# Turning keys in place on VectorE, with zero-padded query weights, in a two-layer decode kernel

## The chip, the cores and the metric

The kernel runs on one core of one Trainium2 chip. The metric is the device time of one execution in microseconds (us), given as the median of several runs. A profile of one execution is shown beside it. In the profile PE is the matrix engine (PEld its weight loads), DVE is VectorE, ACT is ScalarE, POOL is GpSimd and SP is SyncE, which here only issues DMA transfers. "Span" is the profiled execution from its first to its last recorded event.

## The reference, cut to what matters

Two attention blocks and two feed-forward blocks alternate on four tokens (batch B = 4, one position each). The key and value caches are by far the largest operands: 4 x 8 heads x 8192 positions x 128 numbers in bf16, 64 MB for each, and each is read once per attention block.

```python
def _A_ref(x, k_cache, v_cache, wq, wo):          # B=4, Sq=1, D=512, Hq=32, Hkv=8, Sk=8192, Dh=128
    q = (x @ wq).reshape(B, Sq, Hq, Dh).transpose(0, 2, 1, 3)
    k = jnp.repeat(k_cache, 4, axis=1)
    v = jnp.repeat(v_cache, 4, axis=1)
    scores = jnp.einsum("bhqd,bhkd->bhqk", q, k) * (Dh ** -0.5)
    p = _softmax(scores, axis=-1)
    o = jnp.einsum("bhqk,bhkd->bhqd", p, v)
    return o.transpose(0, 2, 1, 3).reshape(B, Sq, Hq * Dh) @ wo
...
x = x + _A_ref(_layernorm(x), A_k_cache, A_v_cache, A_wq, A_wo)
x = x + _B_ref(_layernorm(x), B_w_gate, B_w_up, B_w_down)     # silu(x@wg) * (x@wu) @ wd
x = x + _A_ref(_layernorm(x), A_k_cache, A_v_cache, A_wq, A_wo)
x = x + _B_ref(_layernorm(x), B_w_gate, B_w_up, B_w_down)
```

## The kernel before

**Units.** One unit u is a pair of a key/value head and a batch entry (32 units in each of two layers). Its keys are 8192 x 128 numbers and make one transfer of 2 MB into one of six slots of the tile kv; its values make another. In a slot, partition p holds 64 consecutive positions, so column block t (of 64, 128 columns each) is a 128 x 128 matrix with positions on the partitions. Eight column blocks make one of the eight blocks q of a unit.

**Loads.** All transfers are issued by SP (line 93) in the order of load_order: K0, K1, V0, K2, V1, ... K29, V28, K30, K31, V29, V30, V31, then the same for the second layer. The weights of the output projection and of the feed-forward block are put between the first loads. pump issues a load as soon as a slot is free, and finished, called after the last use of a slot, frees it: so a transfer waits until PE has done its last matmul on an older one. Only the very last V is cut into four transfers with semaphores of their own.

**One unit.** A score is a sum over the 128 head dimensions, so these must lie on the partitions of both operands. Per block q, transposes (line 292) turns eight 128 x 128 matrices by PE matmuls against the identity into a PSUM bank, and DVE (line 299) or ACT (line 301), in turn, copies the 128 x 1024 result over the keys in the slot. scores (line 311) then does eight matmuls, one for each column block, with the turned keys as weights and q as the moving operand, 32 columns wide, of which four count. The scores of a unit fill 256 columns of one bank: partition = position within a block, columns = (t, head). The softmax follows in steps: maximum per partition and head on DVE (line 318), a transpose and a second maximum (max_t, lines 323 to 327), the maximum spread to all partitions by a matmul and subtracted by DVE (max_b, lines 334 to 338), exp on ACT (line 340), and the sum by a matmul with ones, a DVE sum and a reciprocal (lsum, lines 344 to 349). pv (line 358) does 64 matmuls with the values as weights and the exponentials as the moving operand, and DVE multiplies by the reciprocal of the sum (line 364). Every fourth unit, out_proj (line 377) adds four heads' share to x.

**Order.** Every engine takes its instructions in the order in which the program gives them. attention(L) writes that order by hand: in step (u, q) PE does the transposes of block q of unit u, the scores of block q-2, one step of the softmax of unit u-1 at q = 2, 4 and 7, a quarter of the pv of unit u-1 at q = 7, and the other three quarters of unit u-2 at q = 0, 1, 2. So the values of unit u are used during the steps of units u+1 and u+2.

**Between the layers.** center and deviation are the layer norm, ffn the feed-forward block, qproj the query projection (line 416, 128 matmuls), which ends with a DVE multiplication that writes qT (line 422). Nothing of the next layer's keys is touched by an engine before qproj is issued.

Of the kernel before, what the change touches and what calls it, by code (L numbers as in the profile page):

```python
# [103 lines left out]
def bass_interleave_layers__gqa_block_cached__swiglu_ffn__decode_kernel(  # L104
# [25 lines left out]
    NB = TT // TB  # L130
    NQ = 4
# [5 lines left out]
    ALL = range(NB)  # L137

    with ExitStack() as es:
# [9 lines left out]
        ones_bf = sb("ones_bf", [P, P], BF16)  # L149
        onesf = sb("onesf", [P, P], FP32)  # L150
        xio = sb("xio", [B, D], BF16)
# [11 lines left out]
        qT = sb("qT", [P, B * Hq + WIDE], BF16)  # L163
        oT = sb("oT", [P, Hq, B], BF16)
        mx = sb("mx", [P, REP], FP32)
        m4 = sb("m4", [REP, 1], FP32)
        dg = sb("dg", [REP, REP], FP32)
        mb = sb("mb", [P, REP], FP32)
        pT = sb("pT", [P, 2, TT * REP + WIDE], BF16)
        lt = sb("lt", [P, REP], FP32)  # L170
        rl = sb("rl", [P, 2, REP], FP32)
        eg = sb("eg", [P, FO * B], FP32)
        rg = sb("rg", [P, FO * B], FP32)
        gr = sb("gr", [P, FO * B], FP32)
        gw = sb("gw", [P, FO * B], FP32)
        hT = sb("hT", [P, FO * B], BF16)
        xoT = sb("xoT", [P, XB], BF16)

# [10 lines left out]
        STG = [2, 3, 4]  # L189
        OBK = [5, 6]  # L190
        MISC = 7
# [19 lines left out]
        T.op("pool", lambda e: e.memset(onesf[:], 1.0), writes=["onesf"])  # L211
        T.op("pool", lambda e: e.memset(ones_bf[:], 1.0), writes=["ones"])
        T.op("dve", lambda e: e.memset(eps_sb[:], EPS), writes=["eps"])
        T.op("dve", lambda e: e.memset(lsc_sb[:], math.log(scale)), writes=["lsc"])
        T.op("dve", lambda e: e.memset(zero_sb[:], 0.0), writes=["zero"])
        T.op("dve", lambda e: e.tensor_copy(identf[:], ident[:]), reads=["ident"], writes=["identf"])
        T.op("dve", lambda e: e.memset(qT[:, B * Hq:], 0.0), writes=["qpad"])
        T.op("dve", lambda e: e.memset(pT[:, :, TT * REP:], 0.0), writes=["pT0", "pT1"])
        nc.scalar.preload_act_table_set("natural_log_exp_and_others")

# [33 lines left out]
        def pump():  # L254
            while issued[0] < len(items) and free:
# [8 lines left out]
                if items[n] == ("V", 1, NU - 1):  # L264
                    w = TT * Dh // NQ
                    n8 = NB // NQ
                    for q in range(NQ):
                        T.dma("sp", kv[:, s, q * w:(q + 1) * w], src[:, q * w:(q + 1) * w], sem_l[q],
                              writes=[f"s{s}.{q * n8 + k}" for k in range(n8)])
                else:  # L270
                    T.dma("sp", kv[:, s, :], src, sem_s[s], writes=[f"s{s}.{q}" for q in ALL])
# [7 lines left out]
        evac_n = [0]  # L279
        EVAC = ["dve", "act"]  # L280
        stg_n = [0]

        def transposes(L, u, blocks):
            s = slot_of["K", L, u]
            for q in blocks:
                bk = STG[stg_n[0] % len(STG)]
                stg_n[0] += 1
                stg = bank_bf(bk)
                key = f"s{s}.{q}"
                for t in range(TB):  # L290
                    c = (q * TB + t) * Dh
                    T.op("pe", lambda e: e.matmul(stg[:, t * P:(t + 1) * P], lhsT=kv[:, s, c:c + Dh], rhs=ident[:],  # L292
                                                  is_transpose=True, start=True, stop=True),
                         reads=[key, "ident"], writes=[f"pb{bk}"], sig=(t == TB - 1))
                dst = kv[:, s, q * TB * Dh:(q + 1) * TB * Dh]
                eng = EVAC[evac_n[0] % len(EVAC)]
                evac_n[0] += 1
                if eng == "dve":
                    T.op("dve", lambda e: e.tensor_copy(dst, stg[:, :]), reads=[f"pb{bk}"], writes=[key])  # L299
                else:  # L300
                    T.op("act", lambda e: e.activation(dst, stg[:, :], ACTF.Copy), reads=[f"pb{bk}"], writes=[key])  # L301


        def scores(L, u, q):
            g, b = unit_gb(u)
            s = slot_of["K", L, u]
            bk = SBK[u % 2]

            c0 = b * Hq + g * REP
            for t in range(q * TB, (q + 1) * TB):  # L310
                T.op("pe", lambda e: e.matmul(bank(bk)[:, t * REP:t * REP + WIDE], lhsT=kv[:, s, t * P:(t + 1) * P],  # L311
                                              rhs=qT[:, c0:c0 + WIDE], start=True, stop=True),
                     reads=[f"s{s}.{q}", "qpad"] + [f"q{g}" for g in range(G)], writes=[f"pb{bk}"],
                     sig=(t % TB == TB - 1))
            if q == NB - 1:
                finished(("K", L, u))
                v = bank(bk)[:, 0:TT * REP].rearrange("p (t h) -> p h t", h=REP)
                T.op("dve", lambda e: e.tensor_reduce(mx[:], v, AX.X, ALU.max), reads=[f"pb{bk}"], writes=["mx"])  # L318

        mbank = bank(MISC)  # L320

        def max_t(u):
            T.op("pe", lambda e: e.matmul(mbank[0:REP, 0:P], lhsT=mx[:], rhs=identf[:], is_transpose=True,  # L323
                                          start=True, stop=True),
                 reads=["mx", "identf"], writes=["pb7"])
            T.op("dve", lambda e: e.tensor_reduce(m4[:], mbank[0:REP, 0:P], AX.X, ALU.max), reads=["pb7"], writes=["m4"])  # L326
            T.op("dve", lambda e: e.tensor_scalar(dg[:], identf[0:REP, 0:REP], m4[:, 0:1], None, op0=ALU.mult),  # L327
                 reads=["m4", "identf"], writes=["dg"])

        def max_b(u):  # L330
            bk = SBK[u % 2]
            sc = bank(bk)[:, 0:TT * REP]
            sc3 = sc.rearrange("p (t h) -> p t h", h=REP)
            T.op("pe", lambda e: e.matmul(mbank[:, 0:REP], lhsT=onesf[0:REP, :], rhs=dg[:], start=True, stop=True),  # L334
                 reads=["dg", "onesf"], writes=["pb7"])
            T.op("dve", lambda e: e.tensor_copy(mb[:], mbank[:, 0:REP]), reads=["pb7"], writes=["mb"])
            m3 = mb[:].unsqueeze(1).to_broadcast([P, TT, REP])
            T.op("dve", lambda e: e.tensor_tensor(sc3, sc3, m3, ALU.subtract),  # L338
                 reads=[f"pb{bk}", "mb"], writes=[f"pb{bk}"])
            T.op("act", lambda e: e.activation(pT[:, u % 2, 0:TT * REP], sc, ACTF.Exp),  # L340
                 reads=[f"pb{bk}"], writes=[f"pT{u % 2}"])

        def lsum(u):
            T.op("pe", lambda e: e.matmul(mbank[:, 0:TT * REP], lhsT=ones_bf[:], rhs=pT[:, u % 2, 0:TT * REP],  # L344
                                          start=True, stop=True),
                 reads=[f"pT{u % 2}", "ones"], writes=["pb7"])
            T.op("dve", lambda e: e.tensor_reduce(lt[:], mbank[:, 0:TT * REP].rearrange("p (t h) -> p h t", h=REP),  # L347
                                                  AX.X, ALU.add), reads=["pb7"], writes=["lt"])
            T.op("dve", lambda e: e.reciprocal(rl[:, u % 2, :], lt[:]), reads=["lt"], writes=[f"rl{u % 2}"])  # L349


        def pv(L, u, blocks):
            g, b = unit_gb(u)
            s = slot_of["V", L, u]
            bk = OBK[u % 2]

            for t in range(blocks[0] * TB, (blocks[-1] + 1) * TB):
                T.op("pe", lambda e: e.matmul(bank(bk)[:, 0:WIDE], lhsT=kv[:, s, t * Dh:(t + 1) * Dh],  # L358
                                              rhs=pT[:, u % 2, t * REP:t * REP + WIDE],
                                              start=(t == 0), stop=(t == TT - 1)),  # L360
                     reads=[f"s{s}.{t // TB}", f"pT{u % 2}"], writes=[f"pb{bk}"], sig=(t % TB == TB - 1))
            if blocks[-1] == NB - 1:
                finished(("V", L, u))
                T.op("dve", lambda e: e.tensor_tensor(oT[:, g * REP:(g + 1) * REP, b], bank(bk)[:, 0:REP],  # L364
                                                      rl[:, u % 2, :], ALU.mult),
                     reads=[f"pb{bk}", f"rl{u % 2}"], writes=["oT"])


        def add_to_x():
            T.op("dve", lambda e: e.tensor_tensor(xT[:], xT[:], mbank[:, 0:XB], ALU.add),  # L370
                 reads=["x", "pb7"], writes=["x"])

        def out_proj(g):
            for nt in range(KT):
                for r in range(REP):
                    h = g * REP + r
                    T.op("pe", lambda e: e.matmul(mbank[:, nt * B:(nt + 1) * B],  # L377
                                                  lhsT=wo_sb[:, h, nt * P:(nt + 1) * P], rhs=oT[:, h, :],
                                                  start=(r == 0), stop=(r == REP - 1)),
                         reads=[f"wo{h // (Hq // 4)}", "oT"], writes=["pb7"], sig=(r == REP - 1))  # L380
# [6 lines left out]
        def center():  # L387
            T.op("dve", lambda e: e.tensor_reduce(xs[:], xT[:].rearrange("p (k b) -> p b k", b=B), AX.X, ALU.add),
                 reads=["x"], writes=["xs"])
            T.op("pe", lambda e: e.matmul(mbank[:, 0:B], lhsT=onesf[:], rhs=xs[:], start=True, stop=True),  # L390
# [153 lines left out]
```

## Time and profile before

| | us |
|---|---|
| median of 3 runs | 708.73 (706.93 to 709.47) |
| the profiled execution | 707.09 |
| its span | 705.3 |
| PE busy | 560.2 (79% of the span) |
| DVE busy | 317.8 (45%) |
| ACT busy | 280.3 (40%) |
| POOL busy | 1.0 |
| HBM read | 282.33 MB, 400 GB/s over the span |
| idle of ACT before the copies of line 301 | 322.4, ended by the transposes |
| idle of DVE before the copies of line 299 | 237.2, ended by the transposes |

How to read it: the profiled execution is 1.8 us longer than its span and 1.6 us shorter than the median. "Busy" is time with a recorded instruction; a busy PE need not be at its peak, since matmuls overlap. The page also cuts the span into 40 slices of 17.6 us and gives for each the bytes moved per second; other views answer for any stretch of time, listing for each engine its busy time, the clock granted to PE (1.00 is full) and the mean busy share of the 16 DMA engines.

### The profile page before, as it was taken

How to read it: one execution, taken by the hardware profiler on the slowest of the kernel's cores; microseconds unless marked ns; L12 is line 12 of the kernel's file. 1: busy time of each engine (PE TensorE's matmuls, PEld its weight loads, DVE VectorE, ACT ScalarE, POOL GpSimd, SP SyncE). 2: the span in 40 equal slices, each digit the busy share in tenths (PEclk: the TensorE clock that was granted, in tenths of full speed). 3: DMA queues.
4: the chain of work that ended last, by engine and by line, in shares of the span. 5: the costliest groups of instructions: out<-in, count | busy, mean ns of one | idle time of the engine just before them, and what ended most of it. 6: DMA issues, size and time to landing. Idle time of an engine off the chain costs nothing.

```text
span 705.3 us, 28511 instructions
## 1 busy us (share of the span) xinstructions
PE 560.2 (79%) x13416; PEld 534.7 (76%) x13416; DVE 317.8 (45%) x828; ACT 280.3 (40%) x331; POOL 1.0 (0%) x8
## 2 busy tenths in 40 slices
PE   3767676697879778878888887888888987888786
PEld 2767666587768777877778887788878977787786
DVE  0434333353445444444443554555455454445443
ACT  1423323343444444434422543444444444344441
POOL 0000000000000000000000000000000000000000
PEclk9978778989999999999986999999899899999997
DMA  9999999999999999999998799999999999999970
GB/s 366 413 409 403 418 420 419 413 425 427 423 423 427 422 426 426 425 423 426 424 423 351 295 427 425 425 426 420 424 421 424 424 426 425 426 422 425 425 321 7
DMA packets 26598, 284.17 MB, mean 403 GB/s; under 512 B 2280, under 2 KB 8176, under 8 KB 9712
## 3 DMA queue, kind: packets, MB, share of 16 engines
q1 hardware_dynamic: 26480, 282.35, 95.5%
q8 instruction: 105, 1.72, 1.0%
q14 instruction: 13, 0.11, 0.0%
HBM read 282.33 MB, written 0.00 MB: 400 GB/s over the span
## 4 chain that ended last, share of the span: by engine, by line
DMA 49%; PE 37%; issue 6%; DVE 4%; ACT 3%; SPq 1%; DVEq 0%
DMA kv<-in_A_k_cache_dram 44%; PE ps L292 17%; PE ps L358 8%; PE ps L311 7%; DMA kv<-in_A_v_cache_dram 5%; ACT kv L301 2%; DVE kv L299 1%; DVE ps L338 1%; PE ps L334 1%; ACT pT L340 1%; PE ps L323 1%; SPq L93 1%; PE ps L344 1%; PE ps L377 1%; PE ps L416 0%
## 5 line engine op out<-in xcount | busy, mean ns | idle before, releaser
L292 PE MATMUL ps<-ident,kv 128*128 128x128 bf16 x4096 | 342.6, 231 | 73.5 <-DMA kv<-in_A_k_cache_dram 60.7
L301 ACT ACTIVATE kv<-ps 128x1024 bf16<-128x1024 bf16 x256 | 257.9, 1023 | 322.4 <-PE ps L292 322.4
L292 PEld LDWEIGHTS ps<-ident,kv 128*128 128x128 bf16 x4096 | 255.4, 103 | 81.2 <-DMA kv<-in_A_k_cache_dram 63.8
L299 DVE COPY kv<-ps 128x1024 bf16<-128x1024 bf16 x256 | 177.0, 691 | 237.2 <-PE ps L292 237.2
L311 PE MATMUL ps<-qT,kv 128*128 128x32 bf16 x4096 | 188.7, 179 | 21.5 <-ACT kv L301 10.2
L311 PEld LDWEIGHTS ps<-qT,kv 128*128 128x128 bf16 x4096 | 162.3, 99 | 29.0 <-ACT kv L301 16.5
L358 PE MATMUL ps<-pT,kv 128*128 128x32 bf16 x4096 | 146.7, 178 | 28.3 <-issue 22.7
L358 PEld LDWEIGHTS ps<-pT,kv 128*128 128x128 bf16 x4096 | 132.6, 97 | 34.9 <-issue 26.3
L340 ACT ACTIVATE pT<-ps 128x256 bf16<-128x256 f32 x64 | 24.5, 383 | 75.2 <-DVE ps L338 75.2
L318 DVE TENSOR_REDUCE mx<-ps 128x4 f32<-128x256 f32 x64 | 27.2, 424 | 45.5 <-PE ps L311 45.2
L347 DVE TENSOR_REDUCE lt<-ps 128x4 f32<-128x256 f32 x64 | 27.2, 424 | 40.9 <-PE ps L344 40.9
L338 DVE TENSOR_TENSOR ps<-ps,mb 128x256 f32<-128x256 f32 x64 | 27.7, 432 | 2.2
L334 PE MATMUL ps<-dg,onesf 4*128 4x4 f32 x128 | 25.3, 265 | 0.5 <-DVE dg L327 0.5
L334 PEld LDWEIGHTS ps<-dg,onesf 4*128 4x128 f32 x128 | 19.7, 191 | 2.7 <-DVE dg L327 0.7
L344 PE MATMUL ps<-pT,ones_bf 128*128 128x256 bf16 x64 | 17.5, 273 | 2.4 <-ACT pT L340 2.3
L323 PE MATMUL ps<-identf,mx 128*4 128x128 f32 x64 | 18.4, 287 | 0.8 <-issue 0.5
L326 DVE TENSOR_REDUCE m<-ps 4x1 f32<-4x128 f32 x64 | 17.2, 269 | 1.0 <-PE ps L323 1.0
L327 DVE TENSOR_SCALAR dg<-identf,m 4x4 f32<-4x4 f32 x64 | 13.9, 217 | 2.3
L364 DVE TENSOR_TENSOR oT<-ps,rl 128x4 bf16<-128x4 f32 x64 | 9.7, 151 | 10.6 <-PE ps L358 10.6
L416 PE MATMUL ps<-xn,wq_sb 128*128 128x4 bf16 x256 | 7.6, 166 | 8.1 <-DMA wq_sb<-in_A_wq_dram 8.1
L416 PEld LDWEIGHTS ps<-xn,wq_sb 128*128 128x128 bf16 x256 | 7.4, 105 | 8.4 <-DMA wq_sb<-in_A_wq_dram 8.4
L349 DVE RECIPROCAL rl<-lt 128x4 f32<-128x4 f32 x64 | 11.4, 178 | 2.2
(54 smaller groups left out, 84.7 us busy)
## 6 DMA issues: line engine op xcount, KB each, us to landing
kv<-in_A_k_cache_dram SPq DMA_DIRECT2D x64, 2048.0 KB, 17.6
kv<-in_A_v_cache_dram SPq DMA_DIRECT2D x63, 2048.0 KB, 20.0
wq_sb<-in_A_wq_dram SPq DMA_DIRECT2D x4, 1024.0 KB, 8.0
wo_sb<-in_A_wo_dram SPq DMA_DIRECT2D x4, 1024.0 KB, 18.7
kv<-in_A_v_cache_dram SPq DMA_DIRECT2D x4, 512.0 KB, 20.6
wg_sb<-in_B_w_gate_dram SPq DMA_DIRECT2D x1, 1792.0 KB, 25.5
wu_sb<-in_B_w_up_dram SPq DMA_DIRECT2D x1, 1792.0 KB, 29.5
wd_sb<-in_B_w_down_dram SPq DMA_DIRECT2D x1, 1792.0 KB, 26.2
```

Source lines behind the costliest of these rows:

```text
L292: T.op("pe", lambda e: e.matmul(stg[:, t * P:(t + 1) * P], lhsT=kv[:, s, c:c + Dh], rhs=ident[:], is_transpose=True, start=True, stop=True ...
L299: T.op("dve", lambda e: e.tensor_copy(dst, stg[:, :]), reads=[f"pb{bk}"], writes=[key])
L301: T.op("act", lambda e: e.activation(dst, stg[:, :], ACTF.Copy), reads=[f"pb{bk}"], writes=[key])
L311: T.op("pe", lambda e: e.matmul(bank(bk)[:, t * REP:t * REP + WIDE], lhsT=kv[:, s, t * P:(t + 1) * P], rhs=qT[:, c0:c0 + WIDE], start=True ...
L318: T.op("dve", lambda e: e.tensor_reduce(mx[:], v, AX.X, ALU.max), reads=[f"pb{bk}"], writes=["mx"])
L323: T.op("pe", lambda e: e.matmul(mbank[0:REP, 0:P], lhsT=mx[:], rhs=identf[:], is_transpose=True, start=True, stop=True), reads=["mx", "ide ...
L334: T.op("pe", lambda e: e.matmul(mbank[:, 0:REP], lhsT=onesf[0:REP, :], rhs=dg[:], start=True, stop=True), reads=["dg", "onesf"], writes=[" ...
L338: T.op("dve", lambda e: e.tensor_tensor(sc3, sc3, m3, ALU.subtract), reads=[f"pb{bk}", "mb"], writes=[f"pb{bk}"])
L340: T.op("act", lambda e: e.activation(pT[:, u % 2, 0:TT * REP], sc, ACTF.Exp), reads=[f"pb{bk}"], writes=[f"pT{u % 2}"])
L344: T.op("pe", lambda e: e.matmul(mbank[:, 0:TT * REP], lhsT=ones_bf[:], rhs=pT[:, u % 2, 0:TT * REP], start=True, stop=True), reads=[f"pT{u ...
L347: T.op("dve", lambda e: e.tensor_reduce(lt[:], mbank[:, 0:TT * REP].rearrange("p (t h) -> p h t", h=REP), AX.X, ALU.add), reads=["pb7"], w ...
L358: T.op("pe", lambda e: e.matmul(bank(bk)[:, 0:WIDE], lhsT=kv[:, s, t * Dh:(t + 1) * Dh], rhs=pT[:, u % 2, t * REP:t * REP + WIDE], start=( ...
```

## The change

Each key block is turned in place by one DVE transpose over 32-bit words (turn): 128 x 512 words, taken in 32 x 32 squares. A word holds two neighbouring head dimensions, and a square turns 32 positions against 32 words; so afterwards partition 32a + j holds, for the positions of partition group a, the words number j of each quarter row. The other half of the sorting, which word belongs to which head dimension, is left to the matmul: scores takes 256 columns of the turned keys as the moving operand (8 column blocks t, 32 positions i, at a step of two elements), once for each of the four combinations of half row and word half (c), and q as weights zq. zq is 128 x 128 with zeros: place_q (POOL) writes the four heads' values of the unit for each c into the columns of each partition group a, masked by quad, and the start column z0 shifts them by 4q, so that block q's scores land on the PSUM partitions 32a + 4q + head. All 32 matmuls of a unit accumulate in one bank. Scores then lie with (position group, block, head) on the partitions and 256 positions along the columns, so maximum and exp are per partition; exp takes the negated maximum as its bias and gives the sum as well. DVE turns the 128 x 256 exponentials back in 32 x 32 squares (turn_p) for the matmuls of the values.

The order is now a list of loads taken in turn: keys(L, u) for a K, values(L, u) for a V. The softmax steps of a unit are queued in `line` with a gap in microseconds, and advance issues them as the matmuls of other units are issued. After qproj, 16 more matmuls and a DVE copy of 128 x 512 bring q into the order of the words (qr). In the feed-forward block after layer 0, three blocks of the next layer's first unit are turned ahead of the last matmuls, and the other five ahead of qproj. ones is now one column, read 128 times; several buffers of the feed-forward block share one tile, and more PSUM banks have a use of their own.

```diff
-        def transposes(L, u, blocks):
...
-                    T.op("pe", lambda e: e.matmul(stg[:, t * P:(t + 1) * P], lhsT=kv[:, s, c:c + Dh], rhs=ident[:],
-                                                  is_transpose=True, start=True, stop=True),
...
-                if eng == "dve":
-                    T.op("dve", lambda e: e.tensor_copy(dst, stg[:, :]), reads=[f"pb{bk}"], writes=[key])
-                else:
-                    T.op("act", lambda e: e.activation(dst, stg[:, :], ACTF.Copy), reads=[f"pb{bk}"], writes=[key])
+        def turn(L, u, q):
+            s = slot_of["K", L, u]
+            w = kv[:, s, q * TB * Dh:(q + 1) * TB * Dh].bitcast(FP32)
+            T.op("dve", lambda e: e.transpose(w, w), reads=[f"s{s}.{q}"], writes=[f"s{s}.{q}"])
+            turned.add((L, u, q))
+        def place_q(u):
+            g, b = unit_gb(u)
+            shape = [P, 4, NA, REP]
+            dst = zq[:, :, ZP:].rearrange("p c (a x) -> p c a x", a=NA)[:, :, :, 0:REP]
+            q4 = qr[:, :, b, g * REP:(g + 1) * REP].unsqueeze(2).to_broadcast(shape)
+            m4_ = quad[:].unsqueeze(1).unsqueeze(3).to_broadcast(shape)
+            T.op("pool", lambda e: e.tensor_tensor(dst, q4, m4_, ALU.mult), reads=SCR + ["quad"], writes=["zq"])
         def scores(L, u, q):
...
-            for t in range(q * TB, (q + 1) * TB):
-                T.op("pe", lambda e: e.matmul(bank(bk)[:, t * REP:t * REP + WIDE], lhsT=kv[:, s, t * P:(t + 1) * P],
-                                              rhs=qT[:, c0:c0 + WIDE], start=True, stop=True),
...
+            w = kv[:, s, q * TB * Dh:(q + 1) * TB * Dh].rearrange("p (t c i e) -> p t c i e", t=TB, c=2, e=2)
+            z0 = ZP - REP * q
+            for c in range(4):
+                T.op("pe", lambda e: e.matmul(bank(bk)[:, 0:SW], lhsT=zq[:, c, z0:z0 + P], rhs=w[:, :, c // 2, :, c % 2],
+                                              start=(q == 0 and c == 0), stop=(q == NB - 1 and c == 3)),
+                     reads=[f"s{s}.{q}", "zq"], writes=[f"pb{bk}"], sig=(c == 3))
...
+        def exps(u):
+            bk = SBK[u % 2]
+            T.op("pe", lambda e: e.matmul(bank(STEP)[:, 0:1], lhsT=mrow,
+                                          rhs=onesf[0:1, :], start=True, stop=True),
+                 reads=["pb", "onesf"], writes=[f"pb{STEP}"])
+            T.op("act", lambda e: e.activation(nm[:], bank(STEP)[:, 0:1], ACTF.Copy), reads=[f"pb{STEP}"], writes=["nm"])
+            T.op("act", lambda e: e.activation(pb[:], bank(bk)[:, 0:SW], ACTF.Exp, bias=nm[:], accum_out=rs[:]),
+                 reads=[f"pb{bk}", "nm"], writes=["pb", "rs"])
+            T.op("act", lambda e: e.activation(rsm[:], head[:], ACTF.Copy, scale=rs[:]), reads=["head", "rs"], writes=["rsm"])
+        def turn_p(u):
+            T.op("dve", lambda e: e.transpose(pT[:, u % 2, 0:SW], pb[:]), reads=["pb"], writes=[f"pT{u % 2}"])
+        def total(u):
+            T.op("pe", lambda e: e.matmul(bank(TOT)[:, 0:REP], lhsT=ones, rhs=rsm[:], start=True, stop=True),
+                 reads=["rsm", "onesf"], writes=[f"pb{TOT}"])
+            T.op("dve", lambda e: e.reciprocal(rl[:, u % 2, :], bank(TOT)[:, 0:REP]), reads=[f"pb{TOT}"],
+                 writes=[f"rl{u % 2}"])
+        def keys(L, u):
+            place_q(u)
+            for q in range(NB):
+                if (L, u, q) not in turned:
+                    turn(L, u, q)
+                scores(L, u, q)
+                advance(0.55)
+            finished(("K", L, u))
...
+            for gap, fn in ((0.6, max_t), (0.6, exps), (0.9, turn_p), (0.2, total)):
+                line.append([gap, u, lambda fn=fn: fn(u)])
+        def values(L, u):
+            flush(u)
...
+                                              rhs=pT[:, u % 2, c0:c0 + WIDE], start=(t == 0), stop=(t == TT - 1)),
...
+                if t % TB == TB - 1 and q < NB - 1:
+                    advance(0.2)
+            finished(("V", L, u))
...
+            if b == B - 1:
+                line.append([0.4, None, lambda: out_proj(g)])
+            advance(0.2)
...
+            pick = ident[:].rearrange("p (c j e) -> p c j e", c=2, e=2)
+            for c in range(4):
+                for a in range(NA):
+                    T.op("pe", lambda e: e.matmul(bank(OUTB)[a * QB:(a + 1) * QB, c * P:(c + 1) * P],
+                                                  lhsT=pick[:, c // 2, :, c % 2],
+                                                  rhs=qT[:].rearrange("p b h -> p (b h)"), start=True, stop=True),
+                         reads=["qT", "ident"], writes=[f"pb{OUTB}"], sig=(a == NA - 1))
+            T.op("dve", lambda e: e.tensor_copy(scr[:], bank(OUTB)), reads=[f"pb{OUTB}"], writes=SCR)
...
+            if not last:
+                for q in range(3):
+                    turn(1, 0, q)
...
+            if L:
+                for q in range(3, NB):
+                    turn(1, 0, q)
+            qproj()
+            for kind, _, u in load_order(L):
+                (keys if kind == "K" else values)(L, u)
+            flush()
```

## The prediction

> **What bounds the kernel now.** First the page's head, slices and queues: who is busy, and where the flow of bytes breaks.
>
> ```profile
> PE 560.2 (79%) x13416; PEld 534.7 (76%) x13416; DVE 317.8 (45%) x828; ACT 280.3 (40%) x331; POOL 1.0 (0%) x8
> ...
> DMA  9999999999999999999998799999999999999970
> GB/s 366 413 409 403 418 420 419 413 425 427 423 423 427 422 426 426 425 423 426 424 423 351 295 427 425 425 426 420 424 421 424 424 426 425 426 422 425 425 321 7
> ...
> q1 hardware_dynamic: 26480, 282.35, 95.5%
> q8 instruction: 105, 1.72, 1.0%
> ```
>
> The transfers are the bound: a flat 423 to 427 GB/s with all DMA engines busy, except at the start, in the middle (351, 295) and at the end (321, 7). A unit's K and V, 2 x 2.097 MB, take 4.19 MB / 0.425 = 9.9 us; no engine needs that long, and PE waits 61 us in all for keys. So faster compute is worth something only where the flow breaks. These two places in windows (columns after the length: PE, PEld, DVE, ACT, POOL busy, granted PE clock, DMA share, GB/s):
>
> ```profile
> 388.00:390.00 2.00, 1.84 (x45) 1.65 (x42) 1.57 (x3) 1.65 (x2) 0.00 (x0) 1.00 0.47 188
> ...
> 394.00:396.00 2.00, 1.70 (x50) 1.51 (x47) 1.01 (x4) 1.39 (x2) 0.00 (x0) 1.00 0.87 360
> 396.00:398.00 2.00, 1.01 (x31) 0.91 (x27) 0.59 (x1) 0.00 (x0) 0.00 (x0) 1.00 0.12 49
> 398.00:400.00 2.00, 2.00 (x66) 1.99 (x62) 1.27 (x3) 1.02 (x1) 0.00 (x0) 1.00 0.54 123
> ...
> 684.00:685.00 1.00, 1.00 (x22) 1.00 (x19) 0.42 (x3) 0.17 (x1) 0.00 (x0) 0.74 0.51 201
> ...
> 687.00:688.00 1.00, 0.79 (x19) 0.62 (x16) 0.69 (x1) 1.00 (x3) 0.00 (x0) 1.00 0.36 147
> 688.00:689.00 1.00, 0.90 (x33) 0.90 (x34) 0.38 (x1) 0.96 (x2) 0.00 (x0) 1.00 0.06 25
> ```
>
> Where no new load comes, the share does not fall to 0 but to about half: from 381 to 390, and from 680.5 to 688. I read: half of the DMA engines finish the same loads 9.5 us and 7.5 us after the others. The slow half is the true bound; in the middle it has nothing to do only from about 394 to 400 (2 x 0.13 + 2 x 0.88 + 2 x 0.46 = 2.9 us). At the end the last data land at 688.0. Last, the timeline of the tail:
>
> ```profile
> 692.27 0.38 ACT L340 ACTIVATE pT<-ps 128x256 bf16<-128x256 f32 x1 [3.31 <-DVE ps L338]
> ...
> 692.83 1.77 PE L358 MATMUL ps<-pT,kv 128*128 128x32 bf16 x64
> ...
> 694.63 0.17 DVE L364 TENSOR_TENSOR oT<-ps,rl 128x4 bf16<-128x4 f32 x1 [0.97 <-PE ps L358]
> ```
>
> When the last values land, the last unit's softmax has not begun (its maxima are turned on PE at 690.29, exp runs at 692.27): 6.6 us pass from 688.0 to 694.63, then 10.7 us of output projection and feed-forward block.
>
> **What the change costs per unit.** *VectorE.* Eight turns of 128 x 512 words, which no row shows. Bounds: below 0.43 us (a row with 256 elements, line 318), above 1.27 (two passes). The slope of two TENSOR_TENSOR rows, 128 elements in 0.292 (line 422) and 256 in 0.432 (line 338), gives 0.71 for 512 and 1.27 for 1024; the 128x1024 bf16 copy (line 299), the same bytes as 512 words, takes 0.691. I take 0.70: 5.6. Beside it: maximum 0.42, second maximum 0.27, its copy about 0.25, turn_p as a 256-element row 0.43, reciprocal 0.18, oT 0.15, a quarter of add_to_x 0.04: 1.8. Together 7.4 of 9.9 us. [...]
>
> *PE.* 64 transposes go, and 64 scores of 32 columns become 32 of 256. A 128-column matmul follows the last by 0.46/8 = 0.057 us at full clock and by 0.85/8 = 0.106 at half; these are chain rows:
>
> ```profile
> 682.37 0.85 PE ps L292 x8
> ...
> 684.99 0.47 PE ps L292 x8
> ```
>
> So 256 columns take 0.115 to 0.21: 3.7 to 6.8 us; the values 1.77, the small steps about 1: 6.5 to 9.6, under 9.9 even at half clock. [...]
>
> *ACT* loses the 1.02 us copies and adds two short ones. *POOL*'s place_q, 64 elements from two operands: no row; between 0.1 us (a one-element MEMSET) and 0.6 (twice the 0.29 of the AFFINE_SELECT over 128 elements). It waits for the last scores of the unit before, and the next scores wait for it, in PE's slack of up to 3 us.
>
> *Queues.* A turn waits for its K at the head of VectorE's queue; behind it stand turn_p and the reciprocal of the unit before. The values that need them are loaded after that K, so nothing is late. SP issues the same loads in the same order, each K slot free about 6 us after landing (turns 5.6, last scores), each V slot 2 us after its K's scores: earlier than now, where the values of u are used during u+1 and u+2. The loads stay 100% busy: in the steady stretch nothing is gained by this, and nothing lost.
>
> **The sum**, against the profiled span of 705.3:
>
> 1. *Tail.* K31 lands three loads ahead of the last V, so its softmax is done. After 688.0: about 0.8 until PE sees it (the first wq piece: bytes complete near 5.2, first matmul 6.03), the last quarter's 16 matmuls 0.55, oT. 694.63 becomes 689.5: **-5.1** (bounds -2.5, half of it, if other work stands before the last values, to -6.5, all of it). The 10.7 us behind it keep their steps, and already run at clock 0.50.
> 2. *Middle.* Layer 0's last V landed near 390 - 6 x 4.95 = 360.5, but its pv ended at 367.15; now about 363. From there to qT 14.4 us as now (367.15 to 381.5), +0.5 for VectorE's turns beside wd and qproj. New on the path: 16 matmuls 0.9 to 1.7, copy of 512 columns 0.7, place_q 0.1 to 0.6, scores 3.7 to 6.8. First slot free at 383.3 to 387.7, where it is 389.1 now (the next load's issue); the second key unit's, turned meanwhile, at 387 to 395, where it is 398.3 now. The slow half works on old loads to 390 and on the first new one to 395: its hole closes, **-2.9** (to -8.4, the slices' whole deficit, if the halves are no lasting thing).
> 3. *Instruction loads.* q8 is PE's: 105 packets for 2 x 13416 records is 256 each. 1.0% x 16 x 705.3 / 105 = 1.07 us of an engine per packet. The built kernel has about 7,370 matmuls (the records count fp32 ones twice), so 58 packets, 47 fewer: 50 engine-us. Over 16 engines 3.1 us, over 8 6.3. That the halves differ by 9.5 + 7.5 = 17 us, near the 105 x 1.07 / 8 = 14 that the packets would make on eight, speaks for eight: **-5.0**, between them, as that is inference.
>
> 705.3 - 13.0 = 692.3, +1.8 around the span: 694.1 against 707.09. The median lay 1.6 above the profiled execution, within the runs' scatter; I say **694.5**.
>
> **Rivals.**
> - *A, the sum* (0.65): 686 (all bounds: -6.5 - 8.4 - 6.3 = -21.2) to 700.
> - *B, only the tail* (0.13): the slow half is slow for another reason and its hole is filled by something else. 705.3 - 5.1 + 1.8 = 702. For: the halves are read from a mean share alone.
> - *C, VectorE becomes the bound* (0.14): at 1.27 us a turn a unit takes 8 x 1.27 + 1.8 = 12.0 us. First K at 18.4, 64 x 12.0 = 766, less the 8 turns made ahead 10, plus 22 between the layers (softmax and values 5, the chain to qT 14.4, matmuls and copy 2.4) and 15.5 at the end: 812, or **814** with what lies around. The loads cease to bound at (9.9 - 1.8)/8 = 1.01 us a turn, and the kernel is slower from 504 T + 171 = 705, T = 1.06. For: no row shows a turn. Against: from 128 to 1024 elements no VectorE row of the attention costs more than 1.1 ns for a further element, which makes 0.71.
> - *D, a turn between 1.01 and 1.07* (0.08): gain and loss cancel, 705 to 711. That the change does nothing otherwise is hardly possible: the tail's softmax has its data 15 us early.
>
> An interval of 686 to 702 holds A and B; with the runs' scatter and half of D: **685 to 706**. Measurement tells 0.5%, 3.5 us, from no change. Faster 0.65 + 0.13 = 0.78, same 0.08, slower 0.14.
>
> **What would show it.** Turns near 0.70 us and VectorE near 475 us busy; PE under 70%, with more time at 0.50; q8 near 58 packets; no window of the middle under 0.8 DMA share for all engines; last pv about 1.5 us after the last data. Wrong, if VectorE's busy share nears 95%, if the GB/s in the flat stretch falls, or if the half-share shoulder keeps its length though q8 shrinks (then step 3 falls to 3).

## The result, and the profile after

The changed kernel takes **768.9 us** (766.45 to 771.67) where the kernel before took 708.91 (706.93 to 709.47) beside it: a ratio of 1.0853, 95% interval 1.0805 to 1.0900. The forecast was 694.5, in a range of 685 to 706: wrong in sign. The profiled execution has a span of 769.9 us. First the head, slices and queues of its page:

```profile
PE 590.7 (77%) x7368; PEld 445.2 (58%) x7368; DVE 422.1 (55%) x960; ACT 70.1 (9%) x267; POOL 19.8 (3%) x75
...
PEclk9967765786776768677558886867767686777765
...
GB/s 366 415 400 415 423 420 405 427 425 429 424 430 425 421 382 378 379 391 366 265 391 124 408 397 357 386 381 380 367 384 392 371 378 389 375 374 375 401 107 3
...
q8 instruction: 58, 0.95, 0.5%
```

The flow of bytes, flat at 425 before, holds for 14 slices and then drops to about 380. By then the loads have run ahead of the engines as far as six slots allow, and from there the compute sets the pace: 4.19 MB at 379 GB/s are 11.06 us a unit, where the transfers alone need 9.9. Yet no engine is full: PE 77%, VectorE 55%. TensorE's granted clock is 0.733 on the mean, where it was 0.905. So something alternates. The groups of instructions say what (busy time, mean ns, then the idle time ahead and what ended it):

```profile
L334 PE MATMUL ps<-kv,zq 128*128 128x256 bf16 x2048 | 403.5, 367 | 155.5 <-DVE kv L314 154.1
...
L314 DVE STREAM_TRANSPOSE kv<-kv 128x512 f32<-128x512 f32 x512 | 322.8, 675 | 10.7 <-DMA kv<-in_A_k_cache_dram 10.7
...
L378 DVE TENSOR_REDUCE mx<-ps 128x1 f32<-128x256 f32 x64 | 27.2, 425 | 121.7 <-PE ps L334 121.7
```

PE waits 154.1 us for turns, VectorE 121.7 us for scores, and VectorE waits hardly at all for keys (10.7): the keys lie in the slots and are not yet turned. The timeline of one unit shows the order (start, duration, engine, line, what ended the wait ahead):

```profile
205.25 0.17 DVE L398 TENSOR_TENSOR oT<-ps,rl 128x4 bf16<-128x4 f32 x1 [0.97 <-PE ps L392]
...
205.33 0.70 DVE L314 STREAM_TRANSPOSE kv<-kv 128x512 f32<-128x512 f32 x1
...
206.09 0.62 PE L334 MATMUL ps<-kv,zq 128*128 128x256 bf16 x4 [0.88 <-DVE kv L314]
...
207.78 0.18 DVE L365 RECIPROCAL rl<-ps 128x4 f32<-128x4 f32 x1 [0.83 <-PE ps L363]
207.88 3.65 DVE L314 STREAM_TRANSPOSE kv<-kv 128x512 f32<-128x512 f32 x6
...
208.62 4.47 PE L334 MATMUL ps<-kv,zq 128*128 128x256 bf16 x24 [0.88 <-DVE kv L314]
...
213.13 0.42 DVE L378 TENSOR_REDUCE mx<-ps 128x1 f32<-128x256 f32 x1 [1.60 <-PE ps L334]
```

Read it as a queue. The first turn of the new keys stands behind oT of the values before, so it cannot start until PE's last value matmul is done; PE then has nothing but scores, which need the turn. The third turn stands behind the reciprocal, which waits for a small matmul of PE that stands behind the scores of block 1. Only then six turns run, and PE's 24 matmuls trail them by one turn and fall behind. PE waits while VectorE begins a unit, and VectorE waits while PE ends it. The windows of the same stretch give the other half (length, PE busy, granted clock, DMA share, GB/s):

```profile
205.00:206.00 1.00, 0.21 (x9) 1.00 1.04 442
206.00:207.00 1.00, 0.62 (x4) 1.00 0.97 401
207.00:208.00 1.00, 0.74 (x6) 1.00 1.04 442
208.00:209.00 1.00, 0.38 (x3) 0.95 1.06 442
209.00:210.00 1.00, 1.00 (x7) 0.50 0.92 377
210.00:211.00 1.00, 1.00 (x7) 0.50 1.08 459
211.00:212.00 1.00, 1.00 (x7) 0.50 1.00 426
212.00:213.00 1.00, 1.00 (x11) 0.84 0.92 393
```

(The number after x counts the matmuls that touch a window, not those that start in it.) In the four microseconds from 205 to 209 PE is busy for 1.95, and the clock stays at 1.00 almost to their end; just when the scores can run at last, it falls to 0.50, for some 3.4 us (0.1, 3 and 0.3 in the last five windows). Fewer than five matmuls start in a microsecond instead of nine: about 16 of the 24 follow the last by 0.213 us instead of 0.11, 1.6 us in this unit. In the next unit the clock falls again. This unit takes 10.16 us from oT to oT; the next, with an output projection, takes 12.24, and the two after it 11.27 and 10.77.

### The profile page after: what moved, and what is told of

The parts are those of the page before. It is cut to its first block, busy times and chain, and to the rows that moved or that the text cites. A ratio compares the mean times of both kernels' runs of the same rounds, so it can differ in the third digit from the quotient of the medians.

```text
span 769.9 us, 16611 instructions
## 1 busy us (share of the span) xinstructions
PE 590.7 (77%) x7368; PEld 445.2 (58%) x7368; DVE 422.1 (55%) x960; ACT 70.1 (9%) x267; POOL 19.8 (3%) x75
## 4 chain that ended last, share of the span: by engine, by line
PE 65%; DVE 20%; DMA 8%; SPq 3%; issue 2%; ACT 0%; POOL 0%; DVEq 0%
PE ps L334 43%; DVE kv L314 14%; PE ps L392 13%; DMA kv<-in_A_k_cache_dram 7%; SPq L93 3%; PE ps L351 3%; DVE pT L360 2%; DMA wq_sb<-in_A_wq_dram 1%; PE ps L339 1%; PE ps L363 1%; DVE rl L365 1%; DVE oT L398 1%; PE ps L451 1%; PE ps L414 1%; PE ps L498 0%
## 5 line engine op out<-in xcount | busy, mean ns | idle before, releaser
L334 PE MATMUL ps<-kv,zq 128*128 128x256 bf16 x2048 | 403.5, 367 | 155.5 <-DVE kv L314 154.1
L334 PEld LDWEIGHTS ps<-kv,zq 128*128 128x128 bf16 x2048 | 239.9, 127 | 280.3 <-DVE kv L314 194.4
L314 DVE STREAM_TRANSPOSE kv<-kv 128x512 f32<-128x512 f32 x512 | 322.8, 675 | 10.7 <-DMA kv<-in_A_k_cache_dram 10.7
L378 DVE TENSOR_REDUCE mx<-ps 128x1 f32<-128x256 f32 x64 | 27.2, 425 | 121.7 <-PE ps L334 121.7
L398 DVE TENSOR_TENSOR oT<-ps,rl 128x4 bf16<-128x4 f32 x64 | 10.7, 168 | 63.1 <-PE ps L392 63.1
L355 ACT ACTIVATE pb<-ps,nm 128x256 bf16<-128x256 f32 x64 | 30.3, 474 | 2.1
L363 PEld LDWEIGHTS ps<-rsm,onesf 128*128 128x128 f32 x128 | 27.4, 264 | 2.7
L360 DVE STREAM_TRANSPOSE pT<-pb 128x256 bf16<-128x256 bf16 x64 | 26.0, 406 | 4.5 <-ACT pb L355 4.3
L351 PE MATMUL ps<-onesf,pb 1*128 1x1 f32 x128 | 25.2, 263 | 1.6
L351 PEld LDWEIGHTS ps<-onesf,pb 1*128 1x128 f32 x128 | 19.7, 192 | 8.9 <-issue 1.2
L363 PE MATMUL ps<-rsm,onesf 128*128 128x4 f32 x128 | 23.0, 250 | 0.0
```

The costliest lines, as they stand in the source:

```text
L314: T.op("dve", lambda e: e.transpose(w, w), reads=[f"s{s}.{q}"], writes=[f"s{s}.{q}"])
L334: T.op("pe", lambda e: e.matmul(bank(bk)[:, 0:SW], lhsT=zq[:, c, z0:z0 + P], rhs=w[:, :, c // 2, :, c % 2], start=(q == 0 and c == 0), sto ...
L351: T.op("pe", lambda e: e.matmul(bank(STEP)[:, 0:1], lhsT=mrow, rhs=onesf[0:1, :], start=True, stop=True), reads=["pb", "onesf"], writes=[f ...
L355: T.op("act", lambda e: e.activation(pb[:], bank(bk)[:, 0:SW], ACTF.Exp, bias=nm[:], accum_out=rs[:]), reads=[f"pb{bk}", "nm"], writes=["p ...
L360: T.op("dve", lambda e: e.transpose(pT[:, u % 2, 0:SW], pb[:]), reads=["pb"], writes=[f"pT{u % 2}"])
L363: T.op("pe", lambda e: e.matmul(bank(TOT)[:, 0:REP], lhsT=ones, rhs=rsm[:], start=True, stop=True), reads=["rsm", "onesf"], writes=[f"pb{T ...
```

## The experiments

Three readings were open. **A**: the order in VectorE's queue, which lets the two engines run only in turn. **B**: PE's half clock. **C**: simply too much work on VectorE. Where a range is given, the time is a median of four or five runs; without one it is a single run. The kernel before, run beside them, had medians between 707.95 and 709.48.

### Turning ahead of oT; fewer scores; smaller turns; a busy PE

*Three blocks of the next unit's keys are turned ahead of oT:*

```diff
-        def values(L, u):
+        def values(L, u, nxt):                # nxt: the unit of the next K in the list
...
             finished(("V", L, u))
+            for v in nxt:
+                for q in range(AHEAD):        # AHEAD = 3
+                    turn(L, v, q)
             T.op("dve", lambda e: e.tensor_tensor(oT[:, g * REP:(g + 1) * REP, b], bank(bk)[:, 0:REP],
```

> The first three blocks of the next unit's keys are turned at the end of a unit's values, ahead of the oT multiplication on VectorE, instead of behind it. Nothing else changes. Theory A (VectorE's queue order makes the turns of a unit and PE's work on the unit before run one after another, so that the 6.6 us of VectorE and 8 us of PE add up to 11.1 us a unit): the waits of PE for turns (0.97 + 0.58 + 0.96 us in the unit from 205.4) go, a unit falls under the 9.9 us of its transfers, the flow is back at 425 GB/s, 690 to 705 us. Theory B (the loss is PE itself: 256-column score matmuls at half clock, 0.21 us each, fill the unit): PE's work is the same, so at most 20 us are gained, 745 to 770 us. Theory C (VectorE is the bound by its amount of work, 422 us busy): no change, 765 to 770.

Measured: **696.46 us** (695.75 to 697.58), ratio 0.9835 (0.9811 to 0.9858). Its timeline:

```profile
504.92 1.90 DVE L315 STREAM_TRANSPOSE kv<-kv 128x512 f32<-128x512 f32 x3 [2.35 <-DMA kv<-in_A_k_cache_dram]
...
505.69 1.89 PE L335 MATMUL ps<-kv,zq 128*128 128x256 bf16 x8 [2.19 <-DVE kv L315]
506.74 0.13 DVE L402 TENSOR_TENSOR oT<-ps,rl 128x4 bf16<-128x4 f32 x1
```

VectorE now stands at its first turn because the keys have not landed (2.35 us; 103.4 in all, where it was 10.7): the transfers are the bound again. It does the same turns, 512 of 674 ns, so C cannot be the cause of the 72 us; A can.

*Half of the score matmuls are left out (two of four combinations c, so half of each score's sum is missing):*

```diff
-            for c in range(4):
+            for c in range(2):
```

> Only two of the four score matmuls of each block are done (half of the key dimensions is left out of the scores), so PE does 1024 matmuls of 256 columns less; turns and their order stay. Theory A: the waits for the first turns stay (about 2.5 us a unit), the stretch of 24 scores (4.5 to 5.0 us) becomes paced by the six turns (3.65 us and the last block), 0.6 to 1.2 us a unit: 695 to 735 us, with PE waiting for turns longer than the 154 us of the changed kernel, about 300 us. Theory B: 16 x 0.2 = 3.2 us a unit less, the transfers bound again, 690 to 700 us, with waits for turns no longer than now. Theory C: no change, 765 to 770.

Measured: 707.55 us, clock 0.619. Within A's range, above B's. But PE waits 179.7 us for turns, a little more than the 154.1 of the changed kernel and far from the 300 that A expected; with half of the scores the mean clock is 0.619, below the changed kernel's 0.733.

*Each turn takes the first half of its block only (so the other half of the keys is not turned):*

```diff
-            w = kv[:, s, q * TB * Dh:(q + 1) * TB * Dh].bitcast(FP32)
+            w = kv[:, s, q * TB * Dh:(q * TB + TB // 2) * Dh].bitcast(FP32)
```

> Each turn covers only the first half of its block (256 words instead of 512; the other half of the keys is scored unturned), so VectorE does half the work in as many instructions, about 0.34 us each; PE's work and the order stay. Theory A: only the turns that PE waits for count, three a unit: 3 x 0.27 = 0.8 us, about 52 us in all: 710 to 725. Theory B: no change, 760 to 770. Theory C: 512 x 0.27 = 138 us less work on the bound, so the transfers bound again: 690 to 700.

Measured: 699.33 us, a turn 409 ns (340 expected). A's figure was too high. The number is C's, but turning ahead gave about the same gain with all the turns: in a chain that runs in turn, a shorter link helps as much as an overlapped one, so this run cannot tell A from C.

*Twenty matmuls of 256 columns on weights are put into PE's waits, ahead of the scores of blocks 0, 1 and 2; their results go nowhere:*

```diff
+                fill((8, 4, 8)[q] if q < 3 else 0)
                 scores(L, u, q)
```

> Twenty matmuls of 256 columns on constant data into an unused bank are put before the scores of the first three blocks of each unit (8, 4 and 8), where PE waits for turns, to keep its clock up; no result is changed. Theory A: PE's waits are filled and the clock rises towards 1, but the 24 scores then run at VectorE's pace, 6 x 0.61 + 0.5 = 4.2 us instead of 4.5 to 5.0, so 0.3 to 0.8 us a unit less, and the filling itself costs up to 0.5: 735 to 775. Theory B: with 0.115 instead of 0.21 us a score matmul a unit loses 2 us and more: 690 to 720. Theory C: no change.

Measured: 706.75 us, clock 0.954. Here A missed, and B's range holds: more work on PE, nothing moved, and 62 us less. The slices of the clock:

```profile
PEclk9999999999999999999965999999999999999996
```

So the order is not the whole cause. With the clock near 1 the same serial order fits into the transfers' 9.9 us; with the order mended the kernel does so at a mean clock of 0.826. To see what each is worth, the transfers had to be taken out of the way.

### The engines' own loop, with half of the bytes

From the seventh load on only the first half of each K and V is transferred (the engines do all their work, on old data in the second half):

```diff
-                    T.dma("sp", kv[:, s, :], src, sem_s[s], writes=[f"s{s}.{q}" for q in range(NB)])
+                    h = TT * Dh if n < NSLOT else TT * Dh // 2
+                    T.dma("sp", kv[:, s, 0:h], src[:, 0:h], sem_s[s], writes=[f"s{s}.{q}" for q in range(NB)])
```

The kernel after, with half loads:

> The changed kernel, but from the seventh key or value load on only the first half of each is transferred (the second half of a slot keeps old data, so those scores and sums are left out in effect); all instructions stay. A unit's transfers then take about 4.9 us and bound nothing. Theory A+B (the serial loop of VectorE and PE, with PE partly at half clock, is the changed kernel's bound, 11.1 us a unit): as slow as the changed kernel, 755 to 770 us. If something in the transfers made it slow: well below 740.

The same with the twenty matmuls of filler:

> The kernel with the twenty filling matmuls, with half loads as above. It shows the serial loop at a PE clock near 1 without the bound of the transfers. If the clock alone were the cause (theory B), a unit falls far below 9.9 us, 600 us or less in all; by theory A the loop stays serial, about 9.2 to 9.8 us a unit as in the profile of the filled kernel (9.3 from 499.7 to 509), 670 to 700 us.

The same with three blocks turned ahead, without filler:

> The kernel with three blocks turned ahead, with half loads. It shows the loop with VectorE and PE side by side: 8.2 us a unit where data were there (512.3 to 520.5 of its profile), up to 9.5 at half clock: 580 to 660 us by theory A. By theory B (PE's half clock as the main cause) it stays above 680.

And the kernel before, with its transposes on PE:

> The kernel before, in which every load of K or V from the seventh on brings only the first half of its bytes (the computation runs on as it was, on old data in the second half), so that what is left is the time of the engines' own loop. The kernel after with the same cut took 757.1 us. Theory A (the order of the queues and the clock are what the change lost, and the kernel before had neither trouble): PE needs 64 x 0.057 for the transposes, 2 x 1.8 for scores and values and about 1.3 for the small steps, 8.6 us a unit at full clock, 64 x 8.6 = 550 and some 40 to 70 for the start, the middle and the end: 590 to 640. Theory B (the loop of the kernel before was as long as the transfers already, and the change only moved it a little): 680 to 707.

| loop, half of the bytes | us | clock | same kernel, all bytes |
|---|---|---|---|
| after | 757.08 | 0.744 | 768.9 |
| after, filler | 672.36 | 0.970 | 706.75 |
| after, three turns ahead | 553.94 | 0.957 | 696.46 |
| before | 603.49 | 0.950 | 708.91 |

The first, the second and the last of these lie in the ranges expected by A; the kernel with three turns ahead is faster than the 580 to 660 that A expected, and its clock is 0.957, where half clock was allowed for. Halving the bytes takes 12 us off the kernel after and 105 off the kernel before: the one is bound by its own loop, the other by the transfers. With the clock near 1 (0.970) the serial loop costs 84.7 us less (757.1 - 672.4, 1.3 us a unit, near the one unit's 1.6). Overlapping the two engines is worth 203 us (757.1 - 553.9), part of it through the clock, which is 0.957 with the turns ahead, without any filler, where it was 0.744; at about the same clock it is 118 us (672.4 - 553.9), with the filler's own time in it. And the changed kernel's loop, in that order, is 50 us shorter than the one before: as work, the change is a gain.

### How much must be turned ahead

*One block instead of three* (AHEAD = 1):

> As the kernel with three blocks of the next keys turned ahead of oT, but with one block only. It takes away VectorE's stop at oT (0.9 us of PE's wait at a unit's start) and leaves the stop at the reciprocal, which stands ahead of the later turns. Theory A (each stop adds its own wait, and the clock follows PE's waits): the unit of 11.06 us comes down by 0.9 to about 10.2, a little over the transfers' 9.9: 64 x 0.9 = 58 off 768.9, so 705 to 725. Rival B (only the removal of both stops brings PE's clock up; one left is enough to hold it down): 740 to 768. Rival C (the first stop alone was the whole fault): 694 to 700, as with three blocks.

Measured: 730.42 us (730.21 to 732.51), ratio 1.0311 (1.0288 to 1.0333), clock 0.790. Between A's range and B's. The stop at the reciprocal stays (0.83 us of VectorE, and 0.98 and 0.88 of PE around it, in one unit, which takes 8.91 us), and the clock comes up only part of the way (0.733, 0.790, and 0.826 with three blocks). The first stop was not the whole fault: with both gone the time falls by another 34 us. No run takes away the second alone.

*Three blocks ahead of every K, also where a K follows a K* (at the start of a layer, where no values stand between):

```diff
             finished(("K", L, u))
+            for v in nxt:                     # only where the next load is a K
+                for q in range(AHEAD):
+                    turn(L, v, q)
             T.op("dve", lambda e: e.tensor_reduce(mx[:], bank(bk)[:, 0:SW], AX.X, ALU.max),
```

> As the kernel with three blocks turned ahead, and also between two key units that follow each other (K0 and K1, K30 and K31 of each layer), where the first maximum stood ahead of the next turns on VectorE: the hole in the loads from 394 to 400, 3.9 us of the transfers, closes and the last values are reached about 2 us earlier: 689 to 694 us by theory A; no change, 695 to 698, if that hole is not on the path.

Measured: **694.35 us** (693.69 to 694.57), ratio 0.9790 (0.9774 to 0.9806): 2.1% below the kernel before, 2.1 us below the kernel without these turns, and at the edge of the two ranges expected. The second K slot of layer 1 is reused at 394.2 (396.8 with the turns ahead of oT alone, 398.3 before), since the second unit's turns no longer stand behind the first unit's maximum.

### What an instruction packet costs

Both kernels start from the last one and give PE about as much more to do ahead of a unit's first scores: 47 matmuls of 4 columns (81 packets on q8), or 12 of 256 (64 packets).

```diff
+                fill(47 if q == 0 else 0, 4)      # the other: fill(12 if q == 0 else 0, 256)
                 scores(L, u, q)
```

> The kernel with three blocks of every following key turned ahead, and 47 matmuls of 4 columns more per unit on PE ahead of the first scores, in time in which PE waits for the first turn; their results go nowhere. They are 64 x 47 x 2 = 6016 instructions, so about 23.5 more instruction packets of 1.07 us (58 becomes 81 or 82). It tests step 3 of the prediction by itself. If the packets ride on half of the DMA engines, those fall behind by 23.5 x 1.07 / 8 = 3.1 us more: the last data land about 3 us later, the stretch of half share at the end grows from about 4.4 us to 6.2, and the time is 694.4 + 3 = 697.5. If they are spread over all sixteen: 1.6 us, 696.0, with the stretch as it was. If they cost nothing: 694.4. To be read against the twin with few wide matmuls, which takes as much of PE's time.

> The twin of the kernel with 47 small matmuls per unit: 12 matmuls of 256 columns in the same place, about the same 1.4 us of PE, but only 64 x 12 x 2 = 1536 instructions, 6 packets (64 in all). If packets ride on half of the engines: 0.8 us over the kernel without them, 695.2, and 2.3 us below the twin. If on sixteen: 0.4 and 1.2 below the twin. If the twin is as slow as this one, the packets cost nothing and any rise is PE's time. PE's clock should rise alike in both.

Measured: **700.24 us** (699.91 to 700.55) with many small ones, **696.07** (694.17 to 696.75) with few wide ones. The tail of the first, in windows with the same columns as above:

```profile
682.00:683.00 1.00, 1.00 (x27) 0.50 0.49 201
683.00:684.00 1.00, 1.00 (x26) 0.50 0.51 209
684.00:685.00 1.00, 1.00 (x27) 0.53 0.31 111
```

and of the second:

```profile
678.00:679.00 1.00, 1.00 (x46) 1.00 0.51 209
679.00:680.00 1.00, 1.00 (x38) 1.00 0.21 86
```

The last data land about 5 us later in the first of these two executions. The medians differ by 4.17 us for 17 packets, 0.245 us each if the packets are the whole cause; the expectation for half of the engines was 2.3 us and for all sixteen 1.2. That they are the whole cause is not shown, for the twins differ in the clock too: 0.836 and 0.955, where it should have risen alike. The low mean clock does not by itself make a kernel slow (the kernel without filler had 0.844 and 694.35), but in the middle it can. There PE does the first scores of layer 1 at 0.50 until 388 in the first kernel and at 1.00 from 382 in the second; the next load is issued at 388.89 and 384.99, and from 380 to 404 the transfers move 276 and 327 GB/s, which is 2.9 of the 5 us. How much of 4.17 belongs to the packets stays open.

The stretch of half share at the end does grow with the packets: about 4.3 us at 58, 5 at 64, 6.9 at 81, 7.5 at 105. The one in the middle tells nothing, since it ends when the next load comes (5.5, 4, 8.2 and 9.5 us).

## Why the prediction was wrong

**Turn, score matmul, place_q: right.** The turn took 0.675 us (forecast 0.70), place_q 0.292 (0.1 to 0.6), and the 256-column matmuls were 0.11 and 0.213 us apart at full and at half clock (0.115 and 0.21; the second rested on the row of 0.85 us at 682.37, and the windows of the kernel before from 682 to 684 have a granted clock of 0.50). At full clock four score matmuls take 0.62 us, the last of them 0.28, so 0.113 from one to the next; the filler, whose moving operand has no step of two elements, takes 1.03 for eight (0.107) and 1.47 for twelve (0.108), so the step costs next to nothing here. VectorE was busy 422 us, not 475. Rival C, the slower side, was priced at turns above 1.06 us and did not come; the kernel became slower with turns of 0.675.

**Queues: the step that failed.** It said: "behind it stand turn_p and the reciprocal of the unit before. The values that need them are loaded after that K, so nothing is late." It asked who waits behind a turn that waits for its keys. It did not ask what stands ahead of a turn whose keys are there. Ahead stand oT and the reciprocal, both of which wait for PE, while PE waits for the turn. Every figure per unit was added up per engine (VectorE 7.4, PE 6.5 to 9.6) and held against 9.9, which takes it for granted that the engines work side by side. The runs show in its place a loop in which they take turns: PE waits 154.1 us for turns and VectorE 121.7 us for scores, a unit takes 11.06 us instead of 9.9, and moving three turns ahead of oT takes the 768.9 us to 696.46. The sign that the prediction named for itself came: the flow in the flat stretch fell, from 425 to 379 GB/s. The step was checkable before the run: the order of VectorE's instructions in the program is oT, then the first turn, and the waits of both can be read from the code.

**PE "under 9.9 even at half clock": failed too.** PE fell behind and still waited: in the four microseconds from 205 to 209, at the start of the unit shown, it was busy for 1.95, and then the clock was at 0.50 for some 3.4. So the half clock met PE just when the scores of the unit could run. That there would be more time at 0.50, a sign that the prediction named, was the author's estimate, for which it shows no run; it came, with a mean clock of 0.733 where it was 0.905. How long or how fully PE must wait for the clock to fall is not shown. With half of the bytes the price was 84.7 us. It mattered only together with the order: with the order mended, the kernel of 694.35 us runs at a mean clock of 0.844, and its relative with the 12 wide matmuls a unit, at 0.955, is no faster (696.07).

**Tail, middle, instruction loads: the total came out in another kernel than the one predicted, in part by luck.** In the kernel that turns ahead of every K the last data land at 680.0, 8.0 us earlier (forecast 2.9 + 5.0 = 7.9), and the last oT starts 2.2 us later (forecast 1.5, before 6.6), so the tail is worth 4.4 rather than 5.1. The first two slots of layer 1 are free at 386.2 and 394.2, inside the bounds given. The measured 694.35 is the 694.5 of the sum. The division of the 8.0 is not shown: the turns at K after K, which belong to the middle, make 2.1 us; 47 packets would make 3.1 us if spread over sixteen engines, 6.3 over eight, and 11.5, more than the whole, at the 0.245 us that the twins allow at most. That the packets ride on half of the DMA engines is an inference still: the growing stretch at the end speaks for some of the engines, and the profiles do not tell the engines apart. (A slip without effect: 390 - 6 x 4.95 is 360.3, not 360.5.)

## What to carry to other kernels

Before adding busy times per engine, write down for one period the order of each engine's queue and draw who waits for whom: two engines that wait for each other in turn work one after another for that part of the period. When work moves to an engine that has room, put it ahead of that engine's waits for the engine it feeds. And when a loop gets slower with no engine full, take the transfers away (half of the bytes) to see which loop is the bound.

## What the runs showed of the hardware that was not expected

- The clock went to 0.50 after four microseconds (205 to 209) in which PE was busy for 1.95, with no single wait over 1 us (the longest 0.88) in the unit shown, and stayed there for some 3.4 us; matmuls with no use, which kept PE busy, brought the mean clock from 0.733 to 0.954 and the time from 768.9 to 706.75.
- An instruction packet, 256 instructions by the records (2 x 13416 of PE and its weight loads for 105 packets in the kernel before, 2 x 7368 for 58 in the one after, 254 each), takes about 1.07 us of a DMA engine (1.0% of sixteen engines' 705.3 us for the 105 packets of the kernel before), and with 17 packets more a kernel bound by its transfers took 4.17 us more, though not shown to be for the packets alone. PE's own waits put down to "issue" hardly differ between the two kernels: 3.8 us with 81 packets and 3.3 with 64.
